# Attention with normalized q and k, then an MLP: SyncE's order around the transposes, one scaling of k, and ten gates on other engines

## The chip, the cores and the metric

The kernel runs on one core of one Trainium2 chip. Its engines are TensorE (PE in the profile, with its weight loads as PEld), VectorE (DVE), ScalarE (ACT), GpSimd (POOL) and SyncE (SP, which here only issues DMAs). The metric is the device time of one execution in microseconds, lower is better.

## The reference

```python
def _attn_ref(q, k, v, g_q, g_k):
    def rmsnorm(x, g):
        rms = np.sqrt(np.mean(x * x, axis=-1, keepdims=True) + 1e-06)
        return x / rms * g
    q_n, k_n = (rmsnorm(q, g_q), rmsnorm(k, g_k))
    scores = (1.0 / np.sqrt(q.shape[-1])) * np.matmul(q_n, k_n.transpose(0, 1, 3, 2))
    attn = np.exp(scores - np.max(scores, axis=-1, keepdims=True))
    attn = attn / (np.sum(attn, axis=-1, keepdims=True) + 1e-09)
    return np.matmul(attn, v)

def _moe_ref(x, w_in, w_out):
    h = x @ w_in
    g = 0.5 * h * (1.0 + np.tanh(np.sqrt(2.0 / np.pi) * (h + 0.044715 * h * h * h)))
    return g @ w_out
```

q, k and v are 8 batches of 12 heads of 448 rows of 64, in float32. The heads of a row are laid side by side (768 columns), and the 3584 rows go through an MLP with 2048 hidden columns.

## The kernel before

The kernel takes one batch after the other, b = 0 to 7, and overlaps neighbours: while the scores of a batch are made, the output product of the batch before it fills TensorE. A batch from 1 to 7 is written as a list of steps, `STEPS`, a string of tokens that `run` (line 673 on) turns into instructions in the order written. Batches 2, 3 and 4 have lists of their own; 5 and 7 use list 3, and 6 uses list 4. A bar (`|`) parts a list in two:

- the *scores half*: 21 tiles of scores (token `s`: matmuls into PSUM, then ScalarE's exp, line 343), in seven groups of three; additions `a` on VectorE that sum the exps over key tiles (`es`, lines 355 and 357); the output product of the batch before (tokens `A` to `D`, each tile then copied to `osb` and stored by SyncE, line 585); sums over keys (`S`), value products (`x`), reciprocals (`R`), and the product of both (`X`, which gives `xT`).
- the *hidden half*: what is left of these, and the hidden product (`k` tokens: x times w_in, then GELU on ScalarE, line 537).

Heads come in three chunks of four. q and k of a chunk are loaded (`loads`: six DMAs on SyncE's queue, lines 119, 137 and 144), squared, summed (`total`, line 215), normalized (`normed_all`: four instructions on GpSimd, line 238, into `nrmq` and `nrmk`, two buffers each), transposed by two DMAs on SyncE's queue (`transposed`: q at line 285, k at line 281), and k is scaled in place by the product of both gains (`gain`, line 291, on VectorE). `kT` and `qT` have one buffer for the whole chip: the transposes of batch b+1 can only begin when the scores of batch b are done. The raw loads have four buffers, so the load of one chunk waits for the normalization of the chunk that came four before it.

Where all this stands in the order of the queues is said in two ways:

- `m1` holds pairs of a place and a function. A place is a number f (behind the GELU of hidden tile f), `-1` (the token `h-`) or a letter (`hx`, `hs`). `plan` sorts them, keeping the order of those with one place.
- `side` and `late` hold functions for the head and the end of a group of three scores.

At `h-`, `gpsimd_waits` (line 937) has GpSimd copy one element of the batch's last `es`, so that it goes no further before the additions are done; the normalization of batch b+1 stands right behind it.

Most matmuls here use quarters of the array, and the rows' halves take turns on a bank. A `Couple` (line 424 on) runs a first turn, then a *gate*, then a second turn. The gate is a `nop` on some other engine (line 452), which waits for the last matmul of the first turn, and the first matmul of the second turn waits for it. A letter at the end of a token or of an entry of `=...` names the gate's engine: `A` ScalarE, `D` VectorE, `P` GpSimd. So `S10P` is chunk 1's sum over keys, first turn, with its gate on GpSimd, and `S11` is its second turn.

`load_v_piece` (line 170, line 161) has GpSimd issue the load of a part of v for the batch after the next.

Of the kernel before, what the change touches and what calls it, by code (L numbers as in the profile page):

```python
# [16 lines left out]
def kernel(  # L17
# [12 lines left out]
    B, H, S, D = q.shape  # L30
# [14 lines left out]
    NCH = H // CH  # L45
# [603 lines left out]
    for c in range(NCH):  # L649
# [2 lines left out]
    LAST = SEQ[:14] + [(5, "r"), (4, 0), (4, 1), (4, 2), (5, 0), (5, 1), (5, 2)]  # L652
    STEPS = {
# [4 lines left out]
    }  # L658
    work = {}

# [274 lines left out]
    def gpsimd_waits(x):  # L935

        nc.gpsimd.tensor_copy(mark, x)  # L937
# [8 lines left out]
    def normed_all(b, c):  # L946
        for n in "qk":
            for j in range(2):
                normed(b, c, n, j, nc.gpsimd)
# [24 lines left out]
    for b in range(B):  # L974
# [47 lines left out]
            late += [(0, lambda: gain(2, 1)), (2, lambda: gain(2, 2))]  # L1022
        elif b + 1 < B:
            m1.append((-1, lambda: gpsimd_waits(ess[b, HP - 1][:1, 0, :1])))
            for c in range(NCH):
                m1 += [(-1, lambda c=c: normed_all(b + 1, c)),
                       (4 * c + 4, lambda c=c: transposed(b + 1, c))]
            m1 += [(9, lambda: gain(b + 1, 0)), (13, lambda: gain(b + 1, 1))]
            late = [(2, lambda: gain(b + 1, 2))]
        if 1 < b and b + 2 < B:  # L1030
            m1 += [(2, lambda: loads(b + 2, 1)), (6, lambda: loads(b + 2, 2))]
            for c, at in ((0, ("s",) * 4 if b > 2 else ("s", "s", 1, 3)), (1, (9, 10, 11, 12))):
                for i, (n, half) in enumerate((n, half) for n in "qk" for half in range(2)):
                    m1.append((at[i], lambda c=c, n=n, half=half: squared(b + 2, c, n, half)))
                m1 += [((2 if b > 2 else 2, 11)[c], lambda c=c: total(b + 2, c, "q")),
                       ((3 if b > 2 else 5, 13)[c], lambda c=c: total(b + 2, c, "k"))]
            for n in "qk":
                m1.append((13, lambda n=n: square(b + 2, 2, n, nc.gpsimd)))
                early.append((2 + (n == "k"), lambda n=n: total(b + 2, 2, n)))
# [18 lines left out]
        nc.scalar.preload_act_table_set(EXP_SET)  # L1058
        if b + 2 < B:
            hold = [lambda: gpsimd_waits(ess[b + 1, (3, 0)[b]][:1, 0, :1])] if b < 2 else []  # L1060
            at = ((4, 4, 5, 5, 6), (3, 4, 4, 5, 6), (0, 1, 2, 3, 4))[min(b, 2)]
            side += [(at[i], *(hold if i == 0 else ()), lambda i=i: load_v_piece(b + 2, i))
                     for i in range(5)]
            if b + 3 < B:
                side.append((1, lambda: loads(b + 3, 0)))
        state.update(plans=(plan(*side), plan(*early), plan(*late), here), b=b + 1)
        run(b + 1, STEPS[b + 1 if b < 4 else 3 + b % 2].partition("|")[0], m2, call, None)

# [29 lines left out]
```

## Time and profile before

| | |
|---|---|
| median of three runs | 405.51 us (404.07 to 408.17) |
| the profiled execution | 405.13 us |
| its span from the first instruction to the last | 403.3 us |
| TensorE busy | 392.3 us, 97% |
| ScalarE busy | 305.6 us, 76% |
| VectorE busy | 240.9 us, 60% |
| GpSimd busy | 138.4 us, 34% |
| TensorE's granted clock | full speed throughout |

The profile is of one execution. Rows of a timeline give the start in us from the span's start, the length, the engine and line, the operation, `out<-in` by the program's names, and in brackets how long the engine sat idle before it and what ended that. A row of waits reads: who waited, for whom, us in total, how often, the longest. A row of stages gives the stretch, its length, and the busy time and number of instructions of PE, PEld, DVE, ACT and POOL, then the clock, the share of the DMA engines and GB/s. Letters with a q (SPq, POOLq) are an engine's sequencer.

### The profile page before, as it was taken

What the parts mean: (1) busy time and instruction counts of PE and PEld (TensorE: products, weight loads), DVE (VectorE), ACT (ScalarE), POOL (GpSimd) and SP (SyncE); (2) the same over time, 40 slices, a digit from 0 to 9 for tenths busy, and PEclk for the clock granted to TensorE, in tenths of its full rate; (3) what the DMA queues carried; (4) which work ended last, traced back from release to release, by engine and by line L of the source; (5) the groups of instructions that cost most, each with busy time, mean ns of one, the idle gap of its engine ahead of it and who ended that gap; (6) DMA issues with size and microseconds to landing.
All of it is one profiled execution on the core that took longest, in us unless ns stands there. A gap on an engine that the chain in (4) does not pass through costs nothing.

```text
span 403.3 us, 17169 instructions
## 1 busy us (share of the span) xinstructions
PE 392.3 (97%) x7644; PEld 273.0 (68%) x7644; DVE 240.9 (60%) x406; ACT 305.6 (76%) x412; POOL 138.4 (34%) x155
## 2 busy tenths in 40 slices
PE   7899989999999999999999998999999999999996
PEld 3344557677777898766776666766787667966564
DVE  5989839987887437961498314973488411770010
ACT  4997889969997689885998479875998358964400
POOL 6878001252500764065603447037520740000000
PEclk9999999999999999999999999999999999999999
DMA  8999999998891599449981399918980290210022
GB/s 191 225 234 223 205 197 209 232 235 155 208 166 29 158 178 191 98 115 170 183 141 40 92 180 142 195 47 181 156 121 16 74 145 3 81 40 5 2 79 79
DMA packets 98090, 54.65 MB, mean 136 GB/s; under 512 B 63968, under 2 KB 94560, under 8 KB 98016
## 3 DMA queue, kind: packets, MB, share of 16 engines
q1 hardware_dynamic: 71392, 41.69, 47.3%
q0 software_dynamic: 26304, 11.80, 23.0%
q8 instruction: 59, 0.97, 1.0%
q14 instruction: 15, 0.12, 0.1%
q10 hardware_dynamic: 320, 0.07, 0.1%
HBM read 45.61 MB, written 11.01 MB: 140 GB/s over the span
## 4 chain that ended last, share of the span: by engine, by line
PE 88%; SPq 4%; DMA 2%; DVE 2%; ACT 2%; issue 1%; POOL 0%; ACTq 0%; DVEq 0%; POOLq 0%
PE hh L443 25%; PE om L443 16%; PE mm L443 12%; PE o L443 10%; PE sc L336 6%; PE o L557 5%; PE so L443 4%; PE hh L528 4%; PE ox L382 1%; DMA rawk<-in_k_dram 1%; DMA kT<-nrmk 1%; PE sc L322 1%; PE o L382 1%; SPq L285 1%; SPq L144 1%; SPq L119 1%
## 5 line engine op out<-in xcount | busy, mean ns | idle before, releaser
L343 ACT ACTIVATE ex<-sc,shift 128x896 bf16<-128x896 f32 x144 | 137.2, 1023 | 7.7 <-PE sc L336 6.2
L443 PE MATMUL hh<-xT,win 64*64 64x448 bf16 x2304 | 129.3, 349 | 0.0
L443 PEld LDWEIGHTS <-g 64*64 64x64 bf16 x3072 | 105.6, 107 | 27.4 <-issue 1.9
L443 PEld LDWEIGHTS <-win 64*64 64x64 bf16 x2688 | 87.0, 106 | 39.7 <-ACTq L452 10.3
L443 PE MATMUL om<-wout,g 64*64 64x384 bf16 x1664 | 105.0, 323 | 0.1
L443 PE MATMUL o<-wout,g 64*64 64x384 bf16 x704 | 83.0, 323 | 0.6 <-ACT g L537 0.6
L443 PE MATMUL mm<-wout,g 64*64 64x384 bf16 x704 | 83.2, 323 | 0.0
L537 ACT ACTIVATE g<-hh 128x896 bf16<-128x896 f32 x55 | 50.0, 916 | 26.3 <-PE hh L443 24.4
L215 DVE TENSOR_REDUCE ss<-sq 128x14 f32<-128x896 f32 (+4 forms) x45 | 47.8, 1078 | 19.3 <-ACT sq L198 16.9
L336 PE MATMUL sc<-qT,kT 64*64 64x448 bf16 (+1 forms) x540 | 54.8, 352 | 1.9 <-DVE qT L267 1.4
L238 POOL TENSOR_TENSOR nrmq<-rawq,rinv 112x512 bf16<-112x512 f32 x35 | 36.7, 1064 | 34.0 <-DMA qT<-nrmq 28.3
L291 DVE TENSOR_SCALAR kT<-kT,gcol 128x896 bf16<-128x896 bf16 x19 | 13.4, 707 | 51.5 <-DMA kT<-nrmk 51.5
L937 POOL COPY mark<-es 1x1 bf16<-1x1 bf16 x8 | 1.8, 225 | 115.3 <-DVE es L357 97.3
L238 POOL TENSOR_TENSOR nrmk<-rawk,rinv 128x512 bf16<-128x512 f32 (+1 forms) x34 | 31.8, 950 | 3.0 <-ACT rinv L224 2.1
L357 DVE TENSOR_TENSOR es<-ex 128x896 bf16<-128x896 bf16 x42 | 25.8, 614 | 11.7 <-ACT ex L343 11.7
L336 PEld LDWEIGHTS <-kT 64*64 64x64 bf16 (+1 forms) x540 | 23.5, 104 | 12.1 <-issue 4.1
L443 PE MATMUL o<-xT,win 64*64 64x448 bf16 x192 | 30.9, 349 | 0.0
L443 PE MATMUL mm<-xT,win 64*64 64x448 bf16 x192 | 30.9, 349 | 0.0
L357 DVE TENSOR_TENSOR es<-es,ex 128x896 bf16<-128x896 bf16 x42 | 26.0, 620 | 4.3 <-ACT ex L343 2.4
L343 ACT ACTIVATE exr<-sc,shift 128x896 bf16<-128x896 f32 x24 | 24.4, 1018 | 1.2 <-PE sc L322 1.0
L397 DVE STREAM_TRANSPOSE rb<-rc 128x448 f32<-128x448 f32 x34 | 21.9, 645 | 1.1
L443 PEld LDWEIGHTS <-vb 64*64 64x64 bf16 x504 | 16.6, 106 | 6.6 <-ACTq L452 0.8
(120 smaller groups left out, 525.6 us busy)
## 6 DMA issues: line engine op xcount, KB each, us to landing
rawq<-in_q_dram SPq DMA_DIRECT2D x48, 224.0 KB, 4.5
rawk<-in_k_dram SPq DMA_DIRECT2D x48, 192.0 KB, 4.9
vb<-in_v_dram POOLq DMA_DIRECT2D x18, 192.0 KB, 6.1
win<-in_moe_w_in_dram POOLq DMA_DIRECT2D x4, 768.0 KB, 10.8
wout<-in_moe_w_out_dram POOLq DMA_DIRECT2D x4, 768.0 KB, 19.6
out_dram<-osb SPq DMA_DIRECT2D x7, 336.0 KB, 3.4
out_dram<-osb SPq DMA_DIRECT2D x8, 288.0 KB, 2.8
out_dram<-osb SPq DMA_DIRECT2D x8, 240.0 KB, 2.6
```

Source lines behind the costliest of these rows:

```text
L215: nc.vector.reduce_sum(stat(ssq[b % 3], b, c, n, j), view(n, sqs[n, b, c], j), axis=AX.X)
L238: eng.tensor_mul(dst.rearrange("p t a d -> p a t d"), view(n, raws[n, b, c], j), r.to_broadcast(list(r.shape) + [D]),)
L291: nc.vector.tensor_scalar(kT[:, c], kT[:, c], gcol[:, 0:1], None, op0=ALU.mult)
L336: nc.tensor.matmul(sc[o, a, :S], kT[r, c, 4 * j + t, o], qT[b][r, hp], start=True, stop=True,)
L343: nc.scalar.activation(dst, sc[:, :, :S], AF.Exp, scale=scale, bias=shift)
L357: nc.vector.tensor_add(es, ex[:, 0] if t == 1 else es, ex[:, t])
L382: nc.tensor.matmul(o[a * D:(a + 1) * D], w(a), e[:, a], start=(i == 0), stop=(i + 1 == len(steps)),)
L397: nc.vector.transpose(oas["rb", hp], oas["rc"].to_broadcast([128, S // 32, 32]))
L443: self.last = nc.tensor.matmul(self.outs[k][own(m)], w, e, start=not self.begun[k], stop=self.left[k] == 0,)
L528: nc.tensor.matmul(h[i * m:(i + 1) * m, j, :S], win[:, c // 2 + NCH * (c % 2), f * 128 + i * m:f * 128 + (i + 1) * m], xT[b][:, c], start= ...
L537: nc.scalar.activation(g[:, fs[0]:fs[0] + len(fs), (b % 2) * S:(b % 2 + 1) * S], hs1[fs[0]][:, :, :S], AF.Gelu_apprx_tanh)
L557: nc.tensor.matmul(o[j * m:(j + 1) * m, :HD], g[:, f, i * 128 + j * m:i * 128 + (j + 1) * m], wout[:, f, half * HD:(half + 1) * HD], start ...
```

## The change

In batches 2 to 6, for the batch that comes next:

- the token `h-` stands earlier in lists 2, 3 and 4. In list 2 it moves ahead of all but the first steps of the hidden half, in list 3 right behind `hq`, and in list 4 to the head of the hidden half. In lists 2 and 4 some tiles of the output product, with their stores, now come behind it.
- SyncE's transposes of chunks 0 and 1 stand at `h-`, those of chunk 2 behind hidden tile 0 (they stood behind hidden tiles 4, 8 and 12). The loads of chunks 1 and 2 of batch b+2 stand there as well, each ahead of a pair of transposes (they stood behind hidden tiles 2 and 6).
- VectorE's scaling of chunk 1 moves from behind hidden tile 13 to the end of group 1 of the next scores half. Those of chunks 0 and 2 stay.
- for batches b from 2 on, v's five pieces go out in groups 3, 4, 5, 6 and 6 in place of 0 to 4, and the loads of chunk 0 of batch b+3 in group 2 in place of 1.
- ten gates leave GpSimd: in batch 2 `S10` and `S20` go to VectorE and `x20` to ScalarE, in batches 3, 5 and 7 `x10` to VectorE, in batches 4 and 6 `x10` to ScalarE and the gate of the first output tile (`=oADP`, in the tokens `A`) to VectorE.

The tokens of the lists are shown around the places that differ.

```diff
   2:
-  C2 D1 a S10P C1 D1 S11 C1 R1o D1
+  C2 D1 a S10D C1 D1 S11 C1 R1o D1
...
-  | k0:0:0-1! a C1 a C1 D1 k0:1:2-3 k0:1:1-2 D1 k0:1:0-1! D1 C1 k0:0:1-2 S20P D1 k0:0:2-4! S21 R2p x20oP R2oA
+  | k0:0:0-1! a C1 a h- C1 D1 k0:1:2-3 k0:1:1-2 D1 k0:1:0-1! D1 C1 k0:0:1-2 S20D D1 k0:0:2-4! S21 R2p x20oA R2oA
...
-  X2o k1:1:4-5! h- k0:0:4-5! hg
+  X2o k1:1:4-5! k0:0:4-5! hg
   3:
-  R1o C1 R1p x10P s s C1 x11
+  R1o C1 R1p x10D s s C1 x11
...
-  k0:1:3-4 S21 hq x20oA R2o R2pA
+  k0:1:3-4 S21 hq h- x20oA R2o R2pA
...
-  k0:1:0-1 k0:1:2-3! h- k2:1:2-3
+  k0:1:0-1 k0:1:2-3! k2:1:2-3
   4:
-  =oADP,sDDD,sAAD,sADD -K2 s A5 a B1 A2 B1 A1 B1 A1 s A1 B3 A3 B1 s B1 A2 B1 A1 s B2 A2 s a
+  =oADD,sDDD,sAAD,sADD -K2 s A5 a B1 A2 B1 A1 B1 A1 s A1 B3 A3 B1 s B1 A2 B1 A1 s B2 A2 s a
...
-  D1 x10oP a D1 a D1 | hx x11 C2 X1o D1 X1p D1 S20D D2 S21 R2p D5 hs
+  D1 x10oA a D1 a | h- D1 hx x11 C2 X1o D1 X1p D1 S20D D2 S21 R2p D5 hs
...
-  k2:1:4-5 h- k2:1:2-3
+  k2:1:4-5 k2:1:2-3
...
             m1.append((-1, lambda: gpsimd_waits(ess[b, HP - 1][:1, 0, :1])))
+            m1 += [(-1, lambda c=c: normed_all(b + 1, c)) for c in range(NCH)]
             for c in range(NCH):
-                m1 += [(-1, lambda c=c: normed_all(b + 1, c)),
-                       (4 * c + 4, lambda c=c: transposed(b + 1, c))]
-            m1 += [(9, lambda: gain(b + 1, 0)), (13, lambda: gain(b + 1, 1))]
-            late = [(2, lambda: gain(b + 1, 2))]
+                if c < 2 and b + 2 < B:
+                    m1 += [(-1, lambda c=c: loads(b + 2, c + 1))]
+                m1 += [(-1 if c < 2 else 0, lambda c=c: transposed(b + 1, c))]
+            m1 += [(9, lambda: gain(b + 1, 0))]
+            late = [(1, lambda: gain(b + 1, 1)), (2, lambda: gain(b + 1, 2))]
         if 1 < b and b + 2 < B:
-            m1 += [(2, lambda: loads(b + 2, 1)), (6, lambda: loads(b + 2, 2))]
...
-            at = ((4, 4, 5, 5, 6), (3, 4, 4, 5, 6), (0, 1, 2, 3, 4))[min(b, 2)]
+            at = ((4, 4, 5, 5, 6), (3, 4, 4, 5, 6), (3, 4, 5, 6, 6))[min(b, 2)]
...
-                side.append((1, lambda: loads(b + 3, 0)))
+                side.append((2 if b > 1 else 1, lambda: loads(b + 3, 0)))
```

6 rows, old and new, of the table STEPS are left out of this document.

## The prediction

> **What bounds the kernel now.** I read the busy shares first, then the slices of the span, then the chain of work, then the waits of the engines that the chain runs through.
>
> ```profile
> span 403.3 us, 17169 instructions
> PE 392.3 (97%) x7644; PEld 273.0 (68%) x7644; DVE 240.9 (60%) x406; ACT 305.6 (76%) x412; POOL 138.4 (34%) x155
> PE   7899989999999999999999998999999999999996
> ```
>
> TensorE is busy for 392.3 of 403.3 us, so at most 11.0 us are to be had without fewer or shorter matmuls. The slices (10.08 us each) say where those 11.0 us lie: the start, the end, and two slices in between that show an 8. The first of the two is the hand-over from batch 0. The second, slice 25 (242 to 252 us), lies in the steady part, on the boundary between batch 4 and batch 5, and the change touches that place. What held TensorE there:
>
> ```profile
> 252.19 0.38 PE L443 MATMUL mm<-es,ones 64*64 64x448 bf16 x2 [1.16 <-DVE es L357]
> ```
>
> The matmuls that sum the keys of batch 5 waited 1.16 us for VectorE's addition `es`. The chain of waits in order of time says why VectorE was late (start, length, what):
>
> ```profile
> 239.84 3.20 SPq L285
> 243.08 4.79 DMA kT<-nrmk
> 247.90 0.45 DVE kT L291
> 248.35 0.99 DVE ss L215
> 249.34 0.55 DVE es L357
> ...
> 251.52 0.62 DVE es L357
> ...
> 252.19 0.38 PE mm L443 x2
> ```
>
> SyncE issues the transposes of chunk 1 at 239.84 and 243.08, k's lands near 247.87, and only then can VectorE scale it (line 291, 0.45 us). VectorE works in order, so the sum of squares `ss` and four additions stand behind that wait. The scaling is the largest wait of VectorE in the whole trace:
>
> ```profile
> DVE kT L291 <- DMA kT<-nrmk: 51.5, 10, 9.6
> ```
>
> 51.5 us in 10 waits. Nearly all of it costs nothing, for VectorE has slack between the batches; one of the ten reached TensorE. To price that one I cut the scores halves of batches 3, 5 and 7, which run the same step list, at ScalarE's table loads (the load of exp to the load of GELU):
>
> ```profile
> 242.10 1.28 ACT L1058 ACT_TABLE_LOAD   x1
> ...
> 242.10:270.91 28.81, 27.64 (x624) 20.03 (x616) 20.73 (x38) 24.59 (x32) 9.37 (x11) 1.00 0.75 133
> 336.01:363.13 27.12, 27.12 (x628) 21.25 (x620) 17.65 (x34) 23.71 (x30) 0.00 (x0) 1.00 0.15 46
> 149.34:176.71 27.37, 27.37 (x622) 21.71 (x617) 20.95 (x38) 24.36 (x32) 8.46 (x11) 1.00 0.69 133
> ```
>
> Batch 5 takes 28.81 us, batch 3 27.37 and batch 7 27.12, with one list of steps. Batch 5 is 1.44 us above batch 3, its nearest likeness (both load and square a coming batch; 7 does not). TensorE sat idle for 28.81 - 27.64 = 1.17 us of it.
>
> **The change, part by part.**
>
> *SyncE's order, and the earlier mark.* In the hidden half of batch 4 SyncE's queue and GpSimd's normalization stand like this:
>
> ```profile
> 226.42 0.79 SPq L585 DMA_DIRECT2D out_dram<-osb  x2
> 227.31 2.00 SPq L119 DMA_DIRECT2D rawq<-in_q_dram  x1
> ...
> 232.35 1.28 SPq L285 DMA_TRANSPOSE qT<-nrmq  x1
> 218.45 0.18 POOL L937 COPY mark<-es 1x1 bf16<-1x1 bf16 x1 [18.07 <-DVE es L357]
> 218.59 2.04 POOL L238 TENSOR_TENSOR nrmq<-rawq,rinv 112x512 bf16<-112x512 f32 x2
> 220.60 1.83 POOL L238 TENSOR_TENSOR nrmk<-rawk,rinv 128x384 bf16<-128x384 f32 x2
> 237.16 2.29 POOL L238 TENSOR_TENSOR nrmq<-rawq,rinv 112x512 bf16<-112x512 f32 x2 [10.92 <-DMA qT<-nrmq]
> ```
>
> Chunk 0 is normalized at 222.43 (220.60 + 1.83), but SyncE reaches the loads only at 227.31, because the store of tile D's output stands ahead of them and leaves at 226.42. With the mark's work ahead of that store, the first load can leave when its buffer is free, at 220.60 (218.59 + 2.04), and the loads of k at 222.43. The six loads take 5.04 us of queue today (227.31 to 232.35); some of that was the wait now spent earlier, so the transposes of chunk 0 leave at about 226 in place of 232.35. GpSimd's chunk 2, which waits 10.92 us for them at 237.16, moves by the same 6 us, and so does the rest: k of chunk 1 lands near 242 in place of 247.87. Batch 2 has such stores ahead of its loads too, batch 6 has no loads left; in batches 3 and 5 SyncE's order stays as it is, since nothing stands between. The stores now go out behind twelve loads and four transposes, and their three buffers are wanted again only in the next scores half; if that cover were gone, a copy to `osb` would wait, with TensorE's next tile behind it.
>
> *The scaling of chunk 1 leaves the boundary.* Today it stands ahead of the first additions; afterwards it stands behind the sixth score of the new batch. Cost: the same 0.45 us of VectorE, now in front of the scores of chunk 1, the eighth score on. Batch 3 shows what room there is:
>
> ```profile
> 154.14 0.63 DVE L357 TENSOR_TENSOR es<-es,ex 128x896 bf16<-128x896 bf16 x1
> 155.27 0.63 DVE L357 TENSOR_TENSOR es<-ex 128x896 bf16<-128x896 bf16 x1 [0.50 <-ACT ex L343]
> 156.33 0.39 PE L336 MATMUL sc<-qT,kT 64*64 64x448 bf16 x4
> ```
>
> VectorE ends an addition at 154.77 and waits 0.50 us ahead of the next; the eighth score is at 156.33. A scaling from 154.77 to 155.22 leaves 1.11 us. I cost it at nothing. These two parts together take the wait out of the boundary: -1.44 us, with 1.17 (the idle time alone) and 1.69 (28.81 - 27.12) as ends.
>
> *Ten gates change engine.* GpSimd will be normalizing, or issuing v, when they come. Three go to VectorE or ScalarE in batch 2, one to VectorE in each of batches 3, 5 and 7, one to ScalarE and one to VectorE (of the first output tile) in 4 and 6. A gate waits for a first turn of matmuls and releases the second; what stands behind it on its new engine waits too. The gates of batch 3 and batch 4, and what runs near them on the new engine and on TensorE:
>
> ```profile
> L452 POOLq EVENT_SEMAPHORE  x1: 17/17/17, 169.5 to 169.5; - x1
> 169.52 0.65 DVE L397 STREAM_TRANSPOSE rb<-rc 128x448 f32<-128x448 f32 x1
> 169.79 0.74 PE L443 MATMUL so<-ex,vb 64*64 64x448 bf16 x12
> L452 POOLq EVENT_SEMAPHORE  x1: 17/17/17, 217.3 to 217.3; - x1
> 216.74 0.99 ACT L343 ACTIVATE ex<-sc,shift 128x896 bf16<-128x896 f32 x1
> 217.45 0.36 PE L443 MATMUL mm<-ex,vb 64*64 64x448 bf16 x2
> L452 POOLq EVENT_SEMAPHORE  x1: 17/17/17, 197.0 to 197.0; - x1
> 196.04 1.08 DVE L215 TENSOR_REDUCE ss<-sq 128x14 f32<-128x896 f32 x1
> ```
>
> The new neighbour is begun by then or just beginning, so the question is whether a gate can pass while its engine still works. Two gates of today that stand on busy engines answer it:
>
> ```profile
> L452 DVEq EVENT_SEMAPHORE  x1: 21/21/21, 123.8 to 123.8; - x1
> 123.49 0.65 DVE L397 STREAM_TRANSPOSE rb<-rc 128x448 f32<-128x448 f32 x1
> L452 ACTq EVENT_SEMAPHORE  x1: 17/17/17, 166.6 to 166.6; - x1
> 165.79 1.00 ACT L343 ACTIVATE ex<-sc,shift 128x896 bf16<-128x896 f32 x1
> ```
>
> Both pass inside the running instruction (123.8 in 123.49 to 124.14, 166.6 in 165.79 to 166.79). So the gates of batches 3, 5 and 7 come 0.05 us later (behind the start at 169.52), inside the 0.3 us until 169.79, and those of 4 and 6 not at all: 0, with +1.94 as the other end, if they waited for the neighbour's end (170.17 against 169.79 is 0.38 three times; 217.73 against 217.45 is 0.28 twice; 197.12 against 197.0 is 0.12 twice). What is queued behind them on VectorE and ScalarE is the next addition, reciprocal or copy to `osb`, held until TensorE has ended the first turn; ScalarE's copy after the gate at 217.3 waits for TensorE in any case. The three in batch 2 I put at nothing by the same rows. Below nothing they can't go, since GpSimd was waiting at these gates already. The Trainium skill speaks against this part: Perfetto Trace Analysis, section Tensor Engine Instruction, says that "ACT/DVE/GPSIMD are strict FIFO"; read to cover a gate, it gives the +1.94, but the two rows above disagree, and its section Sequencer-only Instruction, which lets such an instruction run on the sequencer alone, fits them.
>
> *v's pieces and one chunk's loads in later groups.* GpSimd issues five pieces of about 0.8 us per batch:
>
> ```profile
> L170 POOL DMA_DIRECT2D vb<-in_v_dram x18 | 13.8, 772 | 7.0 <-PE sc L336 4.6 <-PE o L443 2.0 <-issue 0.3
> ```
>
> Between the old groups and the new ones GpSimd had only the gate at 197.0 of batches 4 and 6, which leaves it, so the pieces come at nearly the same time, and v is used only in the batch after the next: 0, either way. The six loads of chunk 0 go one group of three scores later on a queue that is now free some 6 us sooner: 0; what hides them is again the half batch before their squares.
>
> **Sum.** -1.44 + 0 + 0 + 0 = -1.44. The profiled execution took 405.13 us (span 403.3 and 1.8 around it), so it would take 403.7. The median of the runs shown is 405.51, 0.38 above that execution; on its scale the forecast is 404.1.
>
> **Rivals.**
> - *The wait only moves.* VectorE gets free, but the additions are late for another reason, or the transposes land no sooner because all of the queue moves together. For it: four additions and a copy crowd 249.26 to 252.13. Against it: batches 3 and 7 have the same crowd and no gap. Time: 405.5.
> - *Gates wait for their neighbours.* +1.94 against -1.44: 406.0. Against it: the two rows inside running instructions.
> - *The slower side: the scaling comes late at its new place.* In batches 3 to 7, five times, the eighth score needs it. The room is 1.11 us; it decides from there. If VectorE is then behind by a sum of squares (the 0.99 of the chain), a copy and two additions of 0.63, some 2.4 with the scaling's room used up, TensorE waits 2.4 - 1.1 = 1.3 us five times, 6.5 in all: 405.5 - 1.4 + 6.5 = 410.6. For it: VectorE has over 75% of the half batch to do in batch 3 (20.95 of 27.37). Against it: its wait of 0.50 at just that place.
>
> **How the numbers follow.** Chances: forecast 0.66, the wait only moves 0.16, gates 0.09, the late scaling 0.07, a larger gain 0.02. About 1% (4.1 us) is what a measurement of this kernel can tell from no change, with runs from 404.07 to 408.17. The forecast and two of the rivals lie within it. Faster by over 1% would take 4.1 of the 9.8 us that TensorE idles elsewhere, at start and end mostly: 0.04. Slower by over 1% is the late scaling and some share of the gates: 0.10. Range: the low end is the larger gain of 1.69 and runs as far below their median as the lowest shown (1.44): 402.4. The high end is gates at their full price without any gain: 405.5 + 1.9 = 407.4.
>
> **What would show it.** In the changed kernel's trace: no gap of TensorE near 251 us and no 8 in that slice; the scores half of batch 5 at 27.4 in place of 28.8, those of 3 and 7 unchanged; the waits of line 291 well under 51.5; GpSimd's 10.92 before chunk 2 of batch 4 down to about 4; gates on VectorE and ScalarE within 0.1 us of today's. The prediction is wrong if TensorE shows idle time ahead of the eighth score, or ahead of a second turn in batches 2 to 7, or if the step that should fall (28.8 to 27.4) falls and the total does not.

## The result, and the profile after

The changed kernel takes 411.16 us in the median of 19 executions (406.53 to 417.2), the kernel before 406.69 us in 19 beside it (403.96 to 410.27): a ratio of 1.0096, with a 95% interval of 1.0068 to 1.0123. The ratio leaves out executions more than 1.5% longer than the fastest of their kernel, four of the changed kernel's 19. The changed kernel is about 4 us slower, where 1.4 us less was forecast. The profiled execution of the changed kernel happened to be the longest of the 19 (417.2 us), and the second one used below (e1, 414.18 us) the longest of its four. Sizes read from these two lie at the upper end; shorter executions among the experiments (e4 with 406.63 us, e9 with 407.84) show gaps of the same kind.

The page of the changed kernel answers to the first lines quoted of before:

```profile
span 414.5 us, 17175 instructions
PE 395.7 (95%) x7644; PEld 268.3 (65%) x7644; DVE 243.4 (59%) x406; ACT 306.1 (74%) x412; POOL 138.5 (33%) x155
PE   7899989989999996899999999899999999999996
PEclk9999999999999999899999999999999999999999
```

TensorE is busy 3.4 us longer with the same 7644 matmuls, and idle 18.8 us in place of 11.0. Of the slices (10.36 us each, the first is 0), number 25 (259 to 269 us, batch 5 again) shows an 8, and number 15 (155.4 to 165.8 us), a full 9 before, shows a 6. The slice after it has an 8, and a lower granted clock, which no slice of before has. The stages that I had cut for batches 3 and 5 (exp's table load to GELU's; length, then busy time of PE, PEld, DVE, ACT, POOL, then clock, DMA share, GB/s):

```profile
153.06:187.26 34.20, 28.94 (x624) 19.87 (x616) 20.43 (x38) 24.71 (x31) 6.45 (x10) 0.95 0.76 123
252.94:282.12 29.18, 27.43 (x624) 20.05 (x616) 20.34 (x38) 24.57 (x31) 2.34 (x5) 1.00 0.64 109
```

The scores half of batch 3 grew from 27.37 to 34.20 us, that of batch 5 from 28.81 to 29.18. In batch 3 TensorE stood idle for 34.20 - 28.94 = 5.26 us and was busy 28.94 - 27.37 = 1.57 us longer for the same work. The hidden halves are the same to 0.02 us in all runs, and so is batch 7 (27.11 to 27.12), where nothing is loaded any more. The 5.26 us are two gaps in TensorE's timeline:

```profile
166.19 0.38 PE L336 MATMUL sc<-qT,kT 64*64 64x448 bf16 x3 [3.74 <-issue]
168.09 0.58 PE L443 MATMUL mm<-es,ones 64*64 64x448 bf16 x2 [1.52 <-DVEq L452]
```

*The second gap* the chain of waits of the changed kernel explains:

```profile
153.29 0.42 SPq L585
...
154.61 0.45 SPq L585
...
155.16 2.45 SPq L285
...
157.71 10.27 DMA kT<-nrmk
...
168.00 0.04 DVE kT L291
...
168.09 0.58 PE mm L443 x2
```

SyncE issues four stores (line 585), and only behind them the transposes of chunk 2. k's takes 10.27 us to land; in the kernel before, the transposes of that chunk left at 150.09 and 151.43, 0.8 and 2.1 us behind exp's load (here 2.1 and 4.7), and k's landed 6.1 us later:

```profile
150.09 1.24 SPq L285 DMA_TRANSPOSE qT<-nrmq  x1
151.43 1.24 SPq L281 DMA_TRANSPOSE kT<-nrmk  x1
```

The same four stores had left at 129.5 to 131.7 there, some 20 us ahead of these transposes. In the changed kernel VectorE waits for k's transpose with the scaling of chunk 2, and behind that scaling, on VectorE, stands the gate of the sums over keys (`S00oD`). VectorE's timeline of the changed kernel gives the wait:

```profile
168.00 0.45 DVE L291 TENSOR_SCALAR kT<-kT,gcol 128x896 bf16<-128x896 bf16 x1 [5.47 <-DMA kT<-nrmk]
```

*The first gap* has no releaser: "issue" says that TensorE waited for nothing that the profile shows. What it lacked is instructions. The page's list of queues has one that moves them:

```profile
q8 instruction: 59, 0.97, 1.0%
```

59 packets of 16,384 bytes; the two 7644s above make 15,288 instructions of TensorE, 259 to a packet, so I take this queue to be TensorE's. The Trainium skill (Runtime: NRT & Kernel Launch, Instruction fetch mechanics) has blocks of 16 KiB with 256 instructions, which a sequencer fetches by a DMA queue of its own; the trace's 259 is near that. Its packets come every 5.7 us in the median between 100 and 345 us. Their single times in the trace stand here beside TensorE's gaps (us; "after" is the time since the packet before):

```
kernel, batch        packet  after   ended   TensorE resumes   gap
before, 3            155.12    7.2   156.42        -            none
after, 3             162.32   10.7   164.59      166.19         3.74
after, 5             260.98    9.8   262.00      263.41         1.75
e1, 3                160.82    8.7   161.90      163.72         1.32
e1, 5                258.56    9.6   259.71      261.30         1.70
```

Each time TensorE resumes 1.4 to 1.8 us after the end of the packet. A count of TensorE's instructions in the traces (weight loads, matmuls and its sequencer's own) shows that these gaps are block boundaries: exactly 5,313 instructions lie ahead of the gap in batch 3, in the changed kernel and in e1, e2, e4 and e9 alike, and exactly 9,409 ahead of that in batch 5 (changed kernel, e1, e4, e9), 4,096 or 16 times 256 further on. In all 13 profiles the other gaps over 0.11 us between 100 and 395 us lie on the same grid of 256; only the second gap of batch 3, ahead of the gate, does not (5,319).

The count also shows when a block is asked for. Between 100 and 330 us, over all 13 profiles, a packet starts 0.8 us in the median after TensorE has begun the block before it, and a block takes TensorE 5.8 us. In the five rows of the table the packet started 2.3, 5.8, 5.2, 4.3 and 4.8 us after. Packets that started up to 3.5 us after left no gap over 0.1 us, those between 3.5 and 3.7 sometimes did (0.12 us at 3.61 in batch 4 of the kernel before), and later ones always, but for two whose predecessors TensorE ran in part at the lower clock. The packet itself takes about 1 us, 2.27 at most in these rows; what comes late is its start.

In batch 5 the profile names another releaser, and this is a place where its inference misleads:

```profile
263.41 0.38 PE L443 MATMUL mm<-es,ones 64*64 64x448 bf16 x2 [1.75 <-DVE kT L291]
L452 DVEq EVENT_SEMAPHORE  x1: 21/21/21, 264.0 to 264.0; - x1
```

These matmuls read `es` and ones, not `kT`, and the gate on VectorE passed at 264.0, after they had resumed; the packet that ended at 262.00 fits. In e5 (below) the same matmuls run at 251.37, ahead of that scaling at 252.36, so they do not wait for it. The gap of 1.16 us that the kernel before had at this very place was another: its packet had ended 5.2 us earlier, and TensorE did wait for `es`.

The packets are late where data fills the DMA engines. These are the stretches around the gap in the changed kernel, the next to last column being the DMA engines' share (packet time over 16 engines' time, so above 1 packets overlap on an engine):

```profile
155.00:160.00 5.00, 5.00 (x124) 4.12 (x119) 2.24 (x4) 5.00 (x7) 2.28 (x4) 1.00 1.11 164
160.00:165.00 5.00, 2.45 (x57) 1.76 (x48) 2.26 (x3) 2.92 (x4) 0.00 (x0) 1.00 1.80 133
165.00:170.00 5.00, 2.29 (x27) 1.20 (x31) 1.67 (x4) 1.01 (x1) 0.00 (x0) 0.74 1.10 204
```

and of the kernel before, at the same distance from exp's table load:

```profile
151.00:156.00 5.00, 5.00 (x121) 4.14 (x116) 3.23 (x5) 5.00 (x7) 4.65 (x6) 1.00 0.89 147
156.00:161.00 5.00, 5.00 (x126) 4.60 (x117) 4.38 (x8) 5.00 (x8) 0.00 (x0) 1.00 1.34 232
```

In that crowd are v's five pieces (GpSimd issues them from 153.63), the four stores, the transposes of chunk 2 and, from 160.33, the loads of the next chunk 0. The share alone does not decide: 1.34 here, and 1.38 in a later stretch of e5 (167 to 172 us), left no gap. What holds the start of a packet back within such a crowd is not shown. SyncE's timeline shows how slow its own issues get there:

```profile
151.74 3.32 SPq L585 DMA_DIRECT2D out_dram<-osb  x4
155.16 2.45 SPq L285 DMA_TRANSPOSE qT<-nrmq  x1
157.71 2.57 SPq L281 DMA_TRANSPOSE kT<-nrmk  x1
```

A transpose occupied the queue for 1.24 us at this place before.

*The longer busy time* comes last. Stretches of 2 us of e1, the changed kernel's second execution:

```profile
160.00:162.00 2.00, 2.00 (x55) 1.73 (x45) 1.78 (x3) 2.00 (x4) 0.00 (x0) 1.00 2.09 130
162.00:164.00 2.00, 0.68 (x12) 0.11 (x3) 0.48 (x1) 0.87 (x1) 0.00 (x0) 1.00 1.10 105
164.00:166.00 2.00, 0.52 (x11) 0.25 (x12) 0.45 (x1) 1.01 (x1) 0.00 (x0) 0.91 1.34 238
166.00:168.00 2.00, 2.00 (x32) 1.16 (x28) 1.75 (x4) 0.47 (x1) 0.00 (x0) 0.50 1.17 260
168.00:170.00 2.00, 2.00 (x44) 1.26 (x40) 1.93 (x5) 1.17 (x2) 0.00 (x0) 0.74 0.60 197
```

After two idles of 1.32 and 1.48 us within 3.2 us (162.40 to 165.57), the granted clock is 0.50 for about 3.4 us, and 32 matmuls run in 2 us where 55 ran at full clock. In e1 the half is 32.10 us: these 2.80 of idle and 29.30 of work, 1.93 above the 27.37 of before. The Trainium skill (TensorE: Matmul & The Clock Gate, Part 1: The HAM clock gate) has half rate after an idle window of about 3.4 us, and full rate again after a busy one of that length. The trace agrees with the half rate and with its length of 3.4 us, but no idle time here was that long: the drop came although 0.4 us of matmuls parted the two idles. A single gap of 2.13 us in e9 left the clock at full.

### The profile page after: what moved, and what is told of

It is laid out like the page before. It is cut to its first block, busy times and chain, and to the rows that moved or that the text cites. A ratio compares the mean times of both kernels' runs of the same rounds, so it can differ in the third digit from the quotient of the medians.

```text
span 414.5 us, 17175 instructions
## 1 busy us (share of the span) xinstructions
PE 395.7 (95%) x7644; PEld 268.3 (65%) x7644; DVE 243.4 (59%) x406; ACT 306.1 (74%) x412; POOL 138.5 (33%) x155
## 4 chain that ended last, share of the span: by engine, by line
PE 75%; DMA 17%; ACT 3%; SPq 2%; issue 1%; DVE 1%; POOL 0%; ACTq 0%; POOLq 0%; DVEq 0%
PE hh L443 26%; PE om L443 15%; PE mm L443 11%; PE o L443 9%; DMA rawk<-in_k_dram 7%; DMA wout<-in_moe_w_out_dram 6%; PE sc L336 5%; PE o L557 4%; PE so L443 4%; DMA kT<-nrmk 2%; DMA win<-in_moe_w_in_dram 2%; ACT ex L343 1%; ACT g L537 1%; PE sc L322 1%; SPq L285 1%
## 5 line engine op out<-in xcount | busy, mean ns | idle before, releaser
L343 ACT ACTIVATE ex<-sc,shift 128x896 bf16<-128x896 f32 x144 | 137.5, 1020 | 15.9 <-PE sc L336 13.9
L443 PEld LDWEIGHTS <-g 64*64 64x64 bf16 x3072 | 104.1, 107 | 32.0 <-issue 4.3
L443 PEld LDWEIGHTS <-win 64*64 64x64 bf16 x2688 | 84.2, 106 | 44.5 <-ACTq L452 10.5
L443 PE MATMUL om<-wout,g 64*64 64x384 bf16 x1664 | 106.4, 326 | 1.1 <-issue 0.8
L238 POOL TENSOR_TENSOR nrmq<-rawq,rinv 112x512 bf16<-112x512 f32 x35 | 36.7, 1064 | 19.4 <-DMA qT<-nrmq 13.9
L443 PE MATMUL o<-xT,win 64*64 64x448 bf16 x192 | 30.9, 349 | 0.0
L291 DVE TENSOR_SCALAR kT<-kT,gcol 128x896 bf16<-128x896 bf16 x19 | 15.2, 800 | 19.0 <-DMA kT<-nrmk 19.0
```

The source lines that it names most:

```text
L238: eng.tensor_mul(dst.rearrange("p t a d -> p a t d"), view(n, raws[n, b, c], j), r.to_broadcast(list(r.shape) + [D]),)
L291: nc.vector.tensor_scalar(kT[:, c], kT[:, c], gcol[:, 0:1], None, op0=ALU.mult)
L343: nc.scalar.activation(dst, sc[:, :, :S], AF.Exp, scale=scale, bias=shift)
L443: self.last = nc.tensor.matmul(self.outs[k][own(m)], w, e, start=not self.begun[k], stop=self.left[k] == 0,)
```

## The experiments

Theory A: transfers that crowd into the first 15 us of a scores half make TensorE's instructions come late. Theory B: chunk 2's transposes, behind the stores, make its scaling late, and the gate behind it. The rivals of the prediction (gates, scaling) are tested first. Every kernel here computes all of the reference. Ratios are to the kernel before on the same chip, in brackets the 95% interval; its median was 406.86 us beside e1 to e4, 406.21 beside e5 to e8 and 407.00 beside e9 to e11, so medians are compared within these groups only. e1 has four executions, the others ten or eleven. "3" and "5" are the scores halves of batches 3 and 5.

| run | median, us | ratio | span | 3 | 5 |
|---|---|---|---|---|---|
| the kernel before (first profile) | 406.69 | 1 | 403.3 | 27.37 | 28.81 |
| e1 the change again | 411.42 | 1.0131 [1.0071, 1.0190] | 412.4 | 32.10 | 29.14 |
| e2 ten gates only | 408.07 | 1.0013 [0.9978, 1.0047] | 404.0 | 29.00 | 27.12 |
| e3 scaling only | 406.66 | 0.9986 [0.9952, 1.0020] | 405.6 | 28.03 | 27.12 |
| e4 change, chunk 2's transposes at the mark | 407.99 | 1.0063 [1.0026, 1.0100] | 404.7 | 29.01 | 27.99 |
| e5 change, v held | 405.26 | 0.9966 [0.9939, 0.9993] | 402.5 | 27.12 | 27.12 |
| e6 e5 and e4 | 405.37 | 0.9976 [0.9947, 1.0006] | 403.5 | 27.12 | 27.13 |
| e7 e6, chunk 0's loads later | 405.91 | 0.9985 [0.9955, 1.0015] | 406.3 | 27.12 | 27.12 |
| e8 old order, v held, loads later | 406.55 | 0.9994 [0.9960, 1.0028] | 404.4 | 27.12 | 27.13 |
| e9 e5, v twice, once early | 408.90 | 1.0049 [1.0014, 1.0084] | 405.0 | 29.55 | 28.92 |
| e10 e5, v twice, both late | 405.75 | 0.9986 [0.9954, 1.0019] | 404.2 | 27.14 | 27.14 |
| e11 e5 again | 406.39 | 0.9974 [0.9946, 1.0001] | 403.5 | 27.13 | 27.12 |

The scores half of batch 1, which no edit touches, takes 30.9 us (kernel before) to 34.0 us (changed kernel) over these profiles, in some with gaps of the same "issue" kind: a profiled span varies by up to 3.1 us for that alone, and the span column is read with that in mind. Of the 11.2 us between the first two profiled spans, 6.8 lie in the scores half of batch 3 and 3.1 in that of batch 1.

**e1.** The changed kernel as it is.

> The changed kernel once more, for a second trace. Theory A (instruction blocks): the loss lies in the first scores tiles of batches 3 and 5, where v's pieces, the transposes of chunk 2 and the loads of the next chunk 0 leave together, and TensorE stands still because its next block of instructions (queue 8, 16 KB each) comes late: ratio to the kernel before 1.005 to 1.015, gaps of TensorE of 1 to 4 us that end 1.3 to 1.7 us behind the end of a packet of queue 8. Theory B (the queue order): the loss is chunk 2's transposes alone, issued 3 us later behind four stores: a gap only in batch 3, none in batch 5.

Slower again, with a fetch gap (TensorE without instructions) in batches 3 and 5 and the gate's gap in 3. The loss repeats, at the same places, and the gap in batch 5 speaks against B alone.

**e2.** Before, with the ten gates moved.

```diff
-  S10P ... S20P ... x20oP      (list 2)
+  S10D ... S20D ... x20oA
-  x10P                         (list 3)
+  x10D
-  =oADP ... x10oP              (list 4)
+  =oADD ... x10oA
```

> The kernel before with only the ten gates moved off GpSimd. Theories A and B: the gates cost nothing, ratio 0.998 to 1.002, and the gap of 1.16 us in batch 5 stays. Rival C (the gates wait on their new engines): a loss of 2 to 4 us, ratio 1.005 to 1.010.

1.0013, -0.9 to +1.9 us: the gates' full price of +1.94 lies at its very edge, and the excess of the changed kernel is not there. Two things in its profile matter more. Batch 5's half is 27.12, so the 1.16 us wait that I had quoted from before is gone without any edit to the scaling, against what was expected. And batch 3 shows one gap of the fetch kind, in the page's waits:

```profile
PE sc L336 <- issue: 1.6, 1, 1.6
```

So the old order of SyncE is near that edge as well, and passes it in some executions (e3, in that order too, has a fetch gap of 0.61 us in batch 3).

**e3.** Before, with the scaling of chunk 1 in late group 1.

```diff
-            m1 += [(9, lambda: gain(b + 1, 0)), (13, lambda: gain(b + 1, 1))]
-            late = [(2, lambda: gain(b + 1, 2))]
+            m1 += [(9, lambda: gain(b + 1, 0))]
+            late = [(1, lambda: gain(b + 1, 1)), (2, lambda: gain(b + 1, 2))]
```

> The kernel before with only the scaling of chunk 1 at the end of group 1. By the step of the prediction: the gap of 1.16 us in batch 5 is gone and 1.2 to 1.7 us with it, ratio 0.996 to 0.997. Rival D (late scaling): TensorE waits ahead of the eighth score, ratio above 1.003.

0.9986, not to be told from no change, nor from the forecast's -1.44 us (0.9965). There is no loss in it: the rival of the late scaling (+6.5 us) falls.

**e4.** The changed kernel with chunk 2's transposes at the mark too, ahead of the stores.

```diff
-                m1 += [(-1 if c < 2 else 0, lambda c=c: transposed(b + 1, c))]
+                m1 += [(-1, lambda c=c: transposed(b + 1, c))]
```

> The changed kernel with the transposes of chunk 2 at the mark too, so that they leave ahead of the four stores. Theory B: they land some 5 us sooner in batch 3, the loss is gone, ratio 0.995 to 1.000. Theory A: v's pieces and the loads still crowd the same stretch and TensorE's instruction blocks are still late, ratio 1.004 to 1.012.

1.0063: between the change and the kernel before. k's transpose of chunk 2 in batch 3 lands at 151.90, 2.2 us behind exp's load (14.9 in the changed kernel), the gate's gap is gone and the clock stays at full. The fetch gap stays:

```profile
PE sc L336 <- issue: 1.6, 1, 1.6
```

(packets 148.18 and 158.26, 10.1 apart). In the traces B's gap is gone and A's is there without it. What B costs in the medians is open, for the interval overlaps the changed kernel's.

**e5.** The changed kernel, with GpSimd held ahead of v's pieces until the additions of chunk 1's first pair are done, from batch 2 on.

```diff
-            hold = [lambda: gpsimd_waits(ess[b + 1, (3, 0)[b]][:1, 0, :1])] if b < 2 else []
-            at = (..., (3, 4, 5, 6, 6))[min(b, 2)]
+            hold = [lambda: gpsimd_waits(ess[b + 1, (3, 0, 2)[min(b, 2)]][:1, 0, :1])]
+            at = (..., (4, 4, 5, 6, 6))[min(b, 2)]
```

> The changed kernel with one wait more on GpSimd: v's pieces go out only when the sums of the coming batch's third pair are made, some 10 us later. Theory A (instruction blocks late in the crowd of DMAs) and B (chunk 2's transposes late) both expect a gain here, since the crowd loses v: no gap of TensorE that follows an interval of 8 us or more on queue 8, ratio 0.998 to 1.005 by A. By B alone the transposes still leave behind the four stores and VectorE's scaling still holds a gate: one gap of about 1 us in batch 3, ratio 1.003 to 1.008.

0.9966: the whole loss is gone, and a little more, beyond what A let expect. v's pieces in batch 3 now go out at 164.51, 13.9 us behind exp's load, where they went out 0.6 us behind it (153.63). GpSimd's row and the stages of e5:

```profile
164.51 2.32 POOL L170 DMA_DIRECT2D vb<-in_v_dram  x3 [0.33 <-PE so L443]
150.59:177.71 27.12, 27.12 (x624) 21.61 (x616) 20.25 (x38) 24.36 (x31) 6.31 (x11) 1.00 0.74 136
242.96:270.09 27.13, 27.13 (x624) 21.34 (x616) 20.26 (x38) 24.37 (x32) 6.12 (x10) 1.00 0.60 118
```

TensorE has no idle time in either. Chunk 2's transposes still stand behind the stores, and k's lands at 155.45, 3.1 us after it was issued at 152.39, so B's lateness was mostly the crowd as well.

**e6, e7, e8.** Three further orders: e5 with e4's edit; that with the loads of chunk 0 in group 4; and the old order of SyncE with the gates, the scaling, v held and the loads in group 4.

```diff
                 # e7 and e8
-                side.append((2 if b > 1 else 1, lambda: loads(b + 3, 0)))
+                side.append((4 if b > 1 else 1, lambda: loads(b + 3, 0)))
```

> Both repairs, the transposes of chunk 2 at the mark and v held back. A and B together: no gap over 0.4 us from batch 2 to batch 7, ratio 0.993 to 0.998. If the ratio stays above 1.002, something else of the changed order costs time.

> As the run before, and the loads of chunk 0 of the batch after next in group 4, which puts them behind the store of the first output tile. Theory A: the crowd thins once more, the same as the run before or up to 0.3% better, 0.990 to 0.998. If loads so late hold the squares of the next half: a wait of ScalarE for rawq and a ratio above 1.

> The kernel before in SyncE's old order and with the old place of the mark, with the ten gates off GpSimd, the scaling at group 1, v held back and the loads of chunk 0 in group 4. Theory A: instruction blocks are in time here as well, no gap over 0.4 us, ratio 0.992 to 0.998. If this is no better than the run with both repairs, the new order of the mark is worth nothing by itself.

None is measurably better than e5 (0.9976, 0.9985, 0.9994, all intervals overlap); e7 and e8 lie just above what was expected of them. e8 keeps the old order and cannot be told from the others either, so it is not shown that the new order is worth anything. With the loads in group 4, a fetch gap appears in batch 4 instead, in both profiles (0.80 us in e7, behind a packet that came 10.5 us after the one before; 0.42 us in e8, behind one at 10.1): the crowd only moved to another place.

**e9, e10, e11.** The direct test: e5, with the first three of v's pieces loaded twice, the extra time once early and unheld (e9) or behind the hold as well (e10). Same bytes, same instructions. e11 is e5 once more.

```diff
             # e9; in e10 all three at group 6, behind the held ones
+            if b > 1:
+                side += [((3, 4, 4)[i], lambda i=i: load_v_piece(b + 2, i)) for i in range(3)]
```

> The kernel of e5 with the first three of v's pieces loaded twice from batch 2 on: once unheld in groups 3 and 4, as the changed kernel did, and once behind the hold; both write the same values. Theory A (transfers that crowd into the first 15 us of a scores half make TensorE's instructions come late): a gap of 1 us or more that the profile puts to issue comes back in batch 3 or 5, at 155 to 168 or 250 to 265 us, and the time is 1.5 to 5 us above that of e10. Theory B (only the late transposes of chunk 2 and the scaling behind them cost time, and a hold on GpSimd keeps v's pieces away from them): the transposes of chunk 2 land late again and the matmuls of the sums over keys wait for the scaling of chunk 2, with no gap put to issue. Rival (the hold helped by something else than the transfers, such as GpSimd's place in line): no gap, and the time is that of e10 within 0.4%.

> The kernel of e5 with the first three of v's pieces loaded twice, both times behind the hold: as many bytes and as many instructions on GpSimd as e9, but later. Theories A and B: no gap of TensorE between 150 and 330 us that is put to issue, the scores halves of batches 3 and 5 at 27.1, and a time within 0.4% of the kernel before (405 to 407). Rival (more bytes cost time wherever they are moved): the same loss as in e9.

> The kernel of e5 once more, to see whether its small gain repeats: a ratio of 0.994 to 0.999 if it is real, 1.000 or above if it was chance; no gap put to issue after batch 1 in either case.

Early, the gaps are back in TensorE's timeline of e9, at the same two instructions:

```profile
160.07 0.38 PE L336 MATMUL sc<-qT,kT 64*64 64x448 bf16 x3 [2.13 <-issue]
253.81 0.38 PE L443 MATMUL mm<-es,ones 64*64 64x448 bf16 x2 [1.48 <-DVE kT L291]
```

behind packets that came 8.9 and 9.9 us after the one before and ended at 158.51 and 252.21, 1.6 us ahead of each. These two packets started 5.1 and 4.6 us after TensorE had begun the block before; in e10 the same two started 1.7 and 0.9 us after. The medians differ by 408.90 - 405.75 = 3.15 us, and the two stages by 2.41 + 1.78 = 4.19. Late, the same transfers cost nothing: the stages of e10 are

```profile
151.67:178.81 27.14, 27.14 (x624) 21.59 (x616) 20.28 (x38) 24.37 (x32) 8.81 (x14) 1.00 0.94 154
244.04:271.18 27.14, 27.14 (x624) 21.31 (x616) 20.27 (x38) 24.37 (x32) 8.35 (x13) 1.00 0.75 130
```

A DMA share of 0.94 over the whole half is harmless here, and the bytes are not the cost; the time at which they come is. This shows theory A. e11 repeats e5 with 0.9974, an interval that just reaches 1: e5 is very likely faster than the kernel before, by about 0.3%, and by its ratio it beats the changed kernel by more than 1%. Against what was expected, e11's profile has one gap put to issue behind batch 1, of 0.50 us in batch 2.

## Why the prediction was wrong

**The step that failed** is the one on SyncE's order, and in it this sentence: "The stores now go out behind twelve loads and four transposes, and their three buffers are wanted again only in the next scores half". It stands for the reading that the new order costs nothing beyond its gain of 1.44 us; in its place the runs show a loss of about 4 us. I asked who waits for the stores' buffers. I did not ask what stands behind the stores on the same queue: the transposes of chunk 2, whose k VectorE scales ahead of a gate. The same stores had been gone some 20 us before them; now, behind the loads, they leave right ahead of them, in both batches 2 and 4 (in batch 4 at 219.5 to 226.8 before, 247.0 to 248.9 after, with chunk 2's transposes from 249.45). And I did not add up what the DMA engines carry at the start of the next scores half, where v's pieces, stores, chunk 2's transposes and the next loads now meet. The part on v has the same fault: "0, either way" looked at who needs v, not at what v's transfers hinder, and its ground, that the pieces come "at nearly the same time", did not hold either (below). That TensorE's own instructions come by DMA stood in no part of the prediction, though the page lists the queue. The Trainium skill (Runtime: NRT & Kernel Launch, Instruction fetch mechanics) calls the cost of a block's boundary "mostly hidden"; the runs agree for most of the 59 blocks and differ for these, with up to 3.74 us bare.

The terms of the sum, one by one:

- *SyncE's transposes come sooner*: right. In batch 4 GpSimd's chunk 2 starts 11.8 us ahead of exp's load (4.9 before), and its wait is 4.11, as forecast:

```profile
241.18 2.04 POOL L238 TENSOR_TENSOR nrmq<-rawq,rinv 112x512 bf16<-112x512 f32 x2 [4.11 <-DMA qT<-nrmq]
DVE kT L291 <- DMA kT<-nrmk: 19.0, 5, 5.5
```

  The waits of line 291 fell from 51.5 to 19.0 as well. All of this was off the path.
- *The -1.44 of batch 5*: whether moving the scaling gained it can't be told. The half is 27.12 in e2 and in e3, so the wait of 1.16 us also vanished where the scaling had not moved: I had read a term out of one execution that the next one does not show. No median confirms or excludes it (e3).
- *Ten gates at 0*: right as far as e2 can tell, within -0.9 to +1.9 us; and e5, which has the moved gates, shows no idle time of TensorE in batches 3 and 5.
- *v's groups at 0, "at nearly the same time"*: wrong. v's pieces leave right behind GpSimd's squares, and with the earlier mark those are done sooner. In batch 3 v left 2.7 us behind exp's load before and 0.6 us behind it after; in batch 5 it left 4.95 us behind (247.05 against 242.10) and then 3.54 us ahead (249.40 against 252.94), the rows of before and after:

```profile
247.05 2.33 POOL L170 DMA_DIRECT2D vb<-in_v_dram  x3
249.40 2.32 POOL L170 DMA_DIRECT2D vb<-in_v_dram  x3
```

- *The loads of chunk 0 one group later at 0*: not run alone.
- *The slower rival*: its side came true, its mechanism did not. I had chunk 1's scaling late at its new place, with 1.11 us of room. TensorE shows no wait for it. It was chunk 2's, at a place that was not changed, and by a transfer, not by VectorE's load. The rival's 2.4 us was also added up too low: 0.99, a copy of 0.55 (L610 in the same profile) and twice 0.63 make 2.80.

Against a forecast of -1.44 stand, in e1's batch 3: 1.32 us for late instructions, 1.48 for the gate behind chunk 2's scaling, and 1.93 for the lower clock, 4.73 in all; in batch 5 1.70 for late instructions, in place of the 1.17 that TensorE idled there before. In the median of many executions the loss is some 4 us, since the gaps differ from one to the next.

What stays open is what in the crowd holds a packet's start back. The time since the packet before does not tell a gap: 9.1 us left one of 0.12 us in batch 4 of the kernel before, and 8.7 us left 1.32 us in e1's batch 3; the starts after the block before, 3.6 and 4.3 us, are in the right order. Nor do the runs split the loss between A and B exactly, for both come from one crowd. Batch 1 varies in part by the same gaps, up to 1.50 us in the changed kernel and 2.28 in e7; the rest is open.

## What to carry to other kernels

When transfers are moved, add up per stretch what all queues carry, not only who waits for each transfer: a busy TensorE gets its own instructions by DMA too, and starves where data makes them late (here when a packet started more than 3.7 us after TensorE had begun the block before, 0.8 being usual). An idle time of TensorE put to "issue", at a multiple of 256 instructions from the last one, is the sign; look at the instruction queue's packets. The cure is to hold transfers that nobody needs soon (here v's, wanted a batch later) by a wait on some later event, as one copy on GpSimd did.

## What was not expected of the hardware

- TensorE stops for late instruction packets: gaps of 1.3 to 3.7 us, whole multiples of 256 instructions apart, resuming 1.4 to 1.8 us after the packet's end, where packets came 8.7 to 10.7 us apart in place of 5.7.
- Two gaps of 1.3 and 1.5 us within 3.2 us are enough for the granted clock to go to 0.50 for about 3.4 us: 1.9 us more work time.
- A transposing DMA, which took 2.9 to 6.4 us to land in the kernel before, took 10.27 us in the crowd, and its issue 2.57 us in place of 1.24 at that place.
